# Where the MLP products of the plain tokens stand between the fronts, and which queue loads the first turned tokens

## The chip, the cores and the metric

The kernel runs on one core of one Trainium2 chip. The metric is device time in microseconds (us) of one execution. The kernel before took 865.07 us, the median of three runs (863.32, 865.07 and 866.03).

TensorE (PE) multiplies; PEld is its weight load. VectorE (DVE), ScalarE (ACT) and GpSimd (POOL) do the elementwise work, and SyncE (SP), ACT and POOL also start DMAs. Each of these takes its instructions strictly in its own order.

## What is computed

Linear attention with a decay per head, in blocks, then Fourier mixing, a layer norm and an MLP. Cut to what matters:

```
# q, k, v: 4 batches, 8 heads, 768 positions, 64 per head
x = attention(q, k, v, lam)            # reshaped to (4, 768, 512)
mixed = real(fft(fft(x, axis=1), axis=2))
u = x + mixed
un = (u - mean(u)) / sqrt(var(u) + 1e-06)
out = u + maximum(un @ w_ch1, 0) @ w_ch2   # 512 -> 2048 -> 512
```

All products are float32. The weights come as float64 words and are turned into float32 on the chip.

## The kernel before, in words

**Fronts.** For each of the 4 batches there is a front. `attn(b)` runs 6 chunks of 128 positions: the chunk's k and q are turned (L268, L273), multiplied (L292), masked by DVE (L296), multiplied with v (L324) and with the running state (L320), and turned back (L340). Then `fft_ln(b)` folds the chunk results by symmetry, and for that it gathers mirrored rows from DRAM (`mirror_a`, `mirror_b`, L415 to L431; the stores are on ACT's queue, the gathers on POOL's). `fold_a` and `fold_b` are DVE work; the L483 products need them. Then come three groups t = 1, 2, 0: the L496 to L501 products, DVE sums, and `norm(t)`: statistics on DVE (L513, L514), 1/sqrt on POOL (L517, L518), and the normalized rows `un` on DVE (L530).

**Plain and late tokens.** A group is 256 tokens. `ORDER` lists the 12 groups of (batch, group). The first four, `PLAIN`, are turned by TensorE (L535) and go through `mlp`: 16 times four L599 products with a ReLU on ACT or DVE in turns (L605, L607), and L613 products back to 512 columns, added to `u` (L620 to L625). The other eight, `LATE`, are turned by DVE (L540), stored to DRAM in four small stores each half (`utd`, L544, on SP's queue) along with `u` itself (`ud`, L550).

**The end.** After the last front, `combine_weights(0)` forms sums and differences of weight blocks on DVE (L663, tiles `w1s` and `w2s`); `load_u(0)` loads the first two late groups (tile `ur`, L670); `combine_weights(1)` changes two weight blocks in place. Then `late(j)` does two groups at a time with seven block products where eight would be usual (L686, L733), four times, to the end of the program. The first of them needs `ur`, and from its third product on `us`, which DVE makes from `ur` (L676 to L679).

**What sets the order.** Each generator yields an estimate of the work it has just recorded, and `weave` lets a second generator record its work while the first one's clock runs ahead, by a ratio. The ratios come from `t_front`, `t_mlp`, `t_rest` and `t_back` (L800 to L825). The four plain MLPs (`half[0]`, `half[1]`, `mlp(*PLAIN[3])`) are the filler between the steps of the fronts, since a front is a chain from engine to engine. `t_back` is what of these MLPs is to be spent on the fronts; the number taken off it stays behind the last front, and is drained by `run(weave(combine_weights(0), back, 1.5))` and `run(back)`. A scheduler then settles each engine's order; on the chip it is fixed.

Of the kernel before, what the change touches and what calls it, by code (L numbers as in the profile page):

```python
# [76 lines left out]
def kernel(  # L77
# [10 lines left out]
    nc = tc.nc  # L88
# [4 lines left out]
    NC = S // C  # L93
# [45 lines left out]
    def new(pool, shape, tag, **kw):  # L139
        cnt[0] += 1  # L140
        return pool.tile(shape, F32, tag=tag, name=f"{tag}{cnt[0]}", **kw)

    def psum_a(shape):
        return new(pa, shape, "pa")
# [79 lines left out]
    def weights():  # L224

        for h in range(2):
            for f in range(h * DFF // 2, (h + 1) * DFF // 2, WP):
                for c in range(KO):
                    load_weights(w1[:, c, f:f + WP], w1v[:, c, f:f + WP])
                    yield 1.0  # L230
            for c in range(h * FO // 2, (h + 1) * FO // 2):
                load_weights(w2[:, c, :], w2v[:, c, :])
                yield 1.0
# [7 lines left out]
    def attn(b):  # L241

        head = attn_in(b, 0)
        for c in range(NC):
            yield from head
            head = attn_in(b, c + 1) if c < NC - 1 else ()
            yield from attn_out(b, c, head)
# [146 lines left out]
    uts, utd, ud = {}, {}, {}  # L394
# [42 lines left out]
    def fold_b(b):  # L437

        sets = []
        tt = nc.vector.tensor_tensor  # L440
        for a, n in enumerate(BLK):
            fold_x(b, a, n, 0, xs[b, a][0:n], xs[b, HC + a][0:n])
            e, o = eo[b][a]
            nc.scalar.copy(e[0:n, :, HM:HM + 1], e[0:n, :, DM - 1:DM])

            am, bm = e[0:n, :, W:2 * W], o[0:n, :, W:2 * W]
            lo, hi = e[0:n, 0, 0:HM + 1], e[0:n, 1, 0:HM + 1]
            tt(am[:, 0, 0:HM + 1], lo, hi, op=ALU.add)
            tt(am[:, 1, 0:HM + 1], lo, hi, op=ALU.subtract)

            lo, hi = am[:, :, 0:QM], am[:, :, HM:QM:-1]
            tt(e[0:n, :, 0:QM], lo, hi, op=ALU.add)
            tt(e[0:n, :, QM:HM], lo, hi, op=ALU.subtract)
            lo, hi = o[0:n, 0, 1:HM], o[0:n, 1, 1:HM]
            tt(bm[:, 0, 1:HM], lo, hi, op=ALU.subtract)
            tt(bm[:, 1, 1:HM], lo, hi, op=ALU.add)
            lo, hi = bm[:, :, 1:QM + 1], bm[:, :, HM - 1:QM - 1:-1]
            tt(o[0:n, :, 0:QM], lo, hi, op=ALU.subtract)
            tt(o[0:n, :, QM:HM], lo, hi, op=ALU.add)
            sets.append((e, o))  # L460
        eo.pop(b)

        def piece(a, i, n):

            c0 = W + QM if i == 4 else QM * (i % 2)
            return sets[a][i in (2, 3)][0:BLK[a], n, c0:c0 + (1 if i == 4 else QM)]

        return piece

    def fft_ln(b):  # L470
# [1 line left out]
        fold_a(b)  # L472
        yield 3.0
        piece = fold_b(b)
        yield 6.0


        for i in range(5):
# [30 lines left out]
        def norm(g):  # L509
            mv = new(np_, [128, G, 2], "mv")  # L510
            for i in range(G):
                stt = new(np_, [128, 6], "stt")
                nc.vector.bn_stats(stt, xs[b, TT[g][i]])  # L513
                nc.vector.bn_aggr(mv[:, i, :], stt)  # L514
            ve = new(np_, [128, G], "ve")
            rs = new(np_, [128, G], "rs")
            nc.gpsimd.tensor_scalar(ve, mv[:, :, 1], EPS, None, op0=ALU.add)  # L517
            nc.gpsimd.tensor_tensor(rs, ve, mhalf, op=ALU.pow)  # L518
            yield 1.0
            plain = (b, g) in PLAIN  # L520
            if plain:
                ut = uts[b, g] = new(up, [128, KO, G * 128], "ut")
            else:

                to = utd[b, g] = dram.tile([128, KO, G * 128], F32, name=f"utd{b}{g}")
            for i in range(G):
                un = new(np_, [128, DM], "un", bufs=1)
                u = xs[b, TT[g][i]]
                for o, x in ((un[:, 0:HM], u[:, 0:HM]), (un[:, HM:DM], u[:, DM - 1:HM - 1:-1])):
                    nc.vector.tensor_scalar(o, x, mv[:, i, 0:1], rs[:, i:i + 1],  # L530
                                            op0=ALU.subtract, op1=ALU.mult)
                if plain:
                    pt = psum_a([128, KO, 128])
                    for c in range(KO):
                        nc.tensor.transpose(pt[:, c, :], un[:, 128 * c:128 * c + 128], ident)  # L535
                    nc.scalar.copy(ut[:, :, 128 * i:128 * i + 128], pt)
                else:

                    uq = new(ep, [128, DM], "e")
                    nc.vector.transpose(uq, un)  # L540
                    for r in range(0, 128, 32):
                        dst = to[:, :, 128 * i + r:128 * i + r + 32].rearrange("(a d) c n -> d c a n", d=32)
                        src = uq[r:r + 32].rearrange("p (c a n) -> p c a n", c=KO, n=32)
                        nc.sync.dma_start(dst, src)  # L544
                yield 0.7
            if plain:
                return
            for T in TT[g]:
                ud[b, T] = dram.tile([128, DM], F32, name=f"ud{b}{T}")
                nc.sync.dma_start(ud[b, T], xs.pop((b, T)))  # L550
# [31 lines left out]
    PLAIN, LATE = ORDER[:4], ORDER[4:]  # L582
# [80 lines left out]
                V.tensor_tensor(o[:, i:i + n // 2], x[:, i:i + n // 2], y[:, i:i + n // 2], op=op)  # L663
                yield 1.3

    def load_u(j):

        r = s2.u[j] = new(s2.up, [128, 2, KO, G * 128], "ur", bufs=2)
        for h, (b, g) in enumerate(LATE[2 * j:2 * j + 2]):
            nc.sync.dma_start(r[:, h], utd[b, g])  # L670

    def late(j):
        r = s2.u.pop(j)
# [54 lines left out]
        if 2 * j + 2 < len(LATE):  # L728
            load_u(j + 1)
# [36 lines left out]
    def front(b):  # L766
        yield from attn(b)
        yield from fft_ln(b)

    def weave(lead, other, ratio):  # L770

        t_lead = t_other = 0.0
        for d in lead:
            t_lead += d
            while t_other < t_lead * ratio:
                d = next(other, None)
                if d is None:
                    return t_lead + sum(lead)
                t_other += d
                yield d  # L780
            yield d
        return t_lead

    def run(gen):
        return sum(gen)

    def part(gen, n):
        for d in gen:
            yield d
            n -= d  # L790
            if n <= 0:
                return

    def chain(gens):
        for g in gens:
            yield from g

    NW = 2 * KO * DFF // WP
    w = weights()
    t_chunk = 7.3  # L800
    t_front = NC * t_chunk + 10.0 + 7.0 + 5.7 + 3 * 2.4
    t_mlp = FO * 1.7 + G * 4 * 3.4

    def beside(lead, t, other, t_other):
        return weave(lead, part(other, t_other), t_other / t)

    att1, mix = attn(1), fft_ln(0)
    run(beside(attn(0), NC * t_chunk, w, 0.25 * NW))

# [3 lines left out]
    run(beside(part(att1, t_chunk), t_chunk, w, 0.03 * NW))  # L813
    next(mix)
    run(part(att1, 0.5 * t_chunk))
    run(beside(mix, 20.0, beside(att1, 3.5 * t_chunk, w, 0.19 * NW), 0.19 * NW + 2.5 * t_chunk))

    half = [[mlp(b, g, h * FO // 2, (h + 1) * FO // 2) for b, g in PLAIN[:3]] for h in range(2)]
    fr = chain([att1, fft_ln(1)] + [front(b) for b in range(2, B)])
    t_rest, t_back = 3 * t_front - 5 * t_chunk, len(PLAIN) * t_mlp - 25.0  # L820
    t_half = 1.5 * t_mlp
    run(beside(beside(chain(half[0]), t_half, w, 0.5 * NW), t_half + 0.5 * NW, fr, t_rest * t_half / t_back))
    run(w)
# [3 lines left out]
    s2.wp = ctx.enter_context(tc.tile_pool(name="ws", bufs=1, side="left", reuse_waits="tile"))  # L827
    s2.up = ctx.enter_context(tc.tile_pool(name="us", bufs=1, side="left", reuse_waits="tile"))
    s2.u = {}
    load_u(0)  # L830
    run(weave(combine_weights(0), back, 1.5))
    run(back)
    plain_end.close()
# [37 lines left out]
```

## Time and profile before

| | |
|---|---|
| median of three runs | 865.07 us |
| the profiled execution's own time | 862.61 us |
| its span in the profile | 860.2 us |
| mean granted TensorE clock | 0.978 |
| PE busy | 804.9 us (94%) |
| DVE busy | 445.6 us (52%) |
| ACT busy | 181.4 us (21%) |
| POOL busy | 80.3 us (9%) |
| DMA | 68.87 MB, mean 80 GB/s |

Times in the views count from the span's start. In the view of waits, a line names the engine and line that waited, and after the arrow the engine and line whose work ended the wait; then total us, times, longest. In the timeline, a line has start, duration, engine, line, operation, tiles and count, and in brackets the idle time of the engine just before and what ended it. In the view of windows, the columns are the stretch, its length, the busy us of PE, PEld, DVE, ACT and POOL, the granted TensorE clock (1.00 is full speed), the share of DMA time and GB/s.

One thing to know for counting: every float32 product of the program appears twice in the trace. The order of a built program lists 256 L599 products, the profile 512.

### The profile page before, as it was taken

Reading aid. Unit: us, or ns where it says so; the run is one execution under the profiler, and the core shown is the slowest. Engines: PE = TensorE matmul, PEld = TensorE weight load, DVE = VectorE, ACT = ScalarE, POOL = GpSimd, SP = SyncE. Lnnn points to the kernel's source line nnn. Section 1 sums busy time; section 2 is a strip of 40 time slices with the busy share of each in tenths; the row PEclk is TensorE's granted clock in tenths of the full one; section 3 lists DMA queues with packets and bytes.
Section 4 is the critical chain, followed back from the end, with each engine's and each line's share of the span. In section 5 each row is a group of like instructions: output and inputs, shape, how many; then the busy total and the mean of one; then the engine's idle time right before and its main releaser. Section 6 shows DMA issues by size and latency. Waiting matters only on the chain.

```text
span 860.2 us, 11694 instructions
## 1 busy us (share of the span) xinstructions
PE 804.9 (94%) x4608; PEld 643.4 (75%) x4608; DVE 445.6 (52%) x1030; ACT 181.4 (21%) x436; POOL 80.3 (9%) x102
## 2 busy tenths in 40 slices
PE   5977698999999999999983999999999999999998
PEld 4766575767676767678632888888888888888886
DVE  6969988786712683226396553135511553135411
ACT  3653532314412211221100220012100220012100
POOL 2221132010101011111000000000000000000000
PEclk9998899999999999999995999999999999999999
DMA  9967362136724037511136001010111000110010
GB/s 242 251 163 194 98 190 74 50 104 190 184 51 133 32 68 160 127 64 55 31 80 195 1 1 62 37 49 1 50 50 49 1 1 13 38 49 1 1 37 24
DMA packets 126683, 68.87 MB, mean 80 GB/s; under 512 B 111150, under 2 KB 112174, under 8 KB 126630
## 3 DMA queue, kind: packets, MB, share of 16 engines
q1 hardware_dynamic: 121920, 56.72, 25.4%
q0 software_dynamic: 2112, 6.69, 2.4%
q10 hardware_dynamic: 2598, 4.73, 1.5%
q8 instruction: 36, 0.59, 0.3%
q14 instruction: 17, 0.14, 0.1%
HBM read 48.72 MB, written 19.40 MB: 79 GB/s over the span
## 4 chain that ended last, share of the span: by engine, by line
PE 79%; DVE 11%; DMA 3%; issue 3%; ACT 2%; POOL 1%; SPq 1%; DVEq 0%; POOLq 0%
PE p L686 23%; PE p L733 23%; PE pm L599 9%; PE pm L613 8%; PE pa L292 3%; PE pa L483 3%; PE pa L324 3%; DMA x<-xb,ix 2%; PE pa L320 1%; PE pa L340 1%; PE pa L268 1%; DVE sc L296 1%; PE pa L307 1%; PE pa L273 1%; DVE stt L513 1%
## 5 line engine op out<-in xcount | busy, mean ns | idle before, releaser
L599 PE MATMUL pm<-ut,w 128*128 128x256 f32 x512 | 119.8, 383 | 0.0
L613 PE MATMUL pm<-w,hr 128*128 128x512 f32 x256 | 117.3, 603 | 0.0
L686 PE MATMUL p<-ur,w 128*128 128x256 f32 x384 | 96.2, 386 | 17.6 <-DMA ur<-utd 17.6
L599 PEld LDWEIGHTS pm<-ut,w 128*128 128x128 f32 x512 | 94.3, 190 | 14.3 <-issue 2.7
L686 PEld LDWEIGHTS p<-ur,w 128*128 128x128 f32 x384 | 74.6, 194 | 28.8 <-issue 18.4
L613 PEld LDWEIGHTS pm<-w,hr 128*128 128x128 f32 x256 | 47.2, 192 | 49.3 <-issue 48.7
L686 PE MATMUL p<-us,w1s 128*128 128x256 f32 x256 | 66.6, 383 | 0.0
L733 PE MATMUL p<-w,hs 128*128 128x256 f32 x256 | 58.0, 380 | 0.5 <-DVE y L754 0.5
L733 PE MATMUL p<-w,ha 128*128 128x256 f32 x256 | 57.9, 379 | 0.0
L733 PE MATMUL p<-w2s,hs 128*128 128x256 f32 x256 | 57.9, 379 | 0.0
L686 PEld LDWEIGHTS p<-us,w1s 128*128 128x128 f32 x256 | 49.3, 193 | 6.8
L733 PEld LDWEIGHTS p<-w,hs 128*128 128x128 f32 x256 | 48.6, 190 | 7.5 <-DVE y L754 0.9
L733 PEld LDWEIGHTS p<-w2s,hs 128*128 128x128 f32 x256 | 48.7, 190 | 6.6
L733 PEld LDWEIGHTS p<-w,ha 128*128 128x128 f32 x256 | 48.7, 190 | 6.6
L588 POOL DMA_INDIRECT out_dram<-y,ix x12 | 12.6, 1049 | 405.5 <-DVE y L759 352.6
L713 ACT COPY ha<-p 128x256 f32<-128x256 f32 x32 | 11.9, 372 | 176.2 <-PE p L686 176.2
L292 PEld LDWEIGHTS pa<-qT,kT 64*128 64x128 f32 x384 | 28.6, 204 | 16.4 <-ACT qT L275 8.0
L292 PE MATMUL pa<-qT,kT 64*128 64x128 f32 x384 | 33.7, 305 | 6.2 <-ACT qT L275 5.8
L724 DVE TENSOR_TENSOR ha<-p,ha 128x256 f32<-128x256 f32 x32 | 13.6, 425 | 46.5 <-ACT ha L723 46.5
L296 DVE TENSOR_TENSOR sc<-pa,decay 128x512 f32<-128x512 f32 x48 | 31.6, 684 | 11.4 <-PE pa L292 11.2
L324 PE MATMUL pa<-sc,v 128*64 128x128 f32 x384 | 30.7, 286 | 5.1 <-DVE sc L296 5.0
L264 POOL TENSOR_TENSOR kd<-k,decay 128x512 f32<-128x512 f32 x20 | 22.9, 1147 | 115.9 <-PE pa L307 79.5
(144 smaller groups left out, 1140.4 us busy)
## 6 DMA issues: line engine op xcount, KB each, us to landing
raw<-in_moe_w_ch_dram SPq DMA_DIRECT2D x32, 512.0 KB, 4.7
k<-in_k_dram SPq DMA_DIRECT2D x24, 256.0 KB, 4.2
q<-in_q_dram SPq DMA_DIRECT2D x24, 256.0 KB, 5.3
v<-in_v_dram SPq DMA_DIRECT2D x24, 256.0 KB, 3.9
ud<-x SPq DMA_DIRECT2D x16, 256.0 KB, 2.5
utd<-e SPq DMA_DIRECT2D x64, 64.0 KB, 2.2
ur<-utd SPq DMA_DIRECT2D x8, 512.0 KB, 6.7
u<-ud SPq DMA_DIRECT2D x16, 256.0 KB, 2.7
```

Source lines behind the costliest of these rows:

```text
L264: nc.gpsimd.tensor_tensor(kd, kt, kpow, op=ALU.mult)
L292: mm(pss[hi][:, hp, :], lhsT=kT[HD[hi], hp, :], rhs=qT[HD[hi], hp, :], start=True, stop=True)
L296: nc.vector.tensor_tensor(t, pss[hi], decay[:, hi::2, :], op=ALU.mult)
L324: mm(po[HD[hi], hp, :], lhsT=vt[:, 2 * hp + hi, :], rhs=sc[hi][:, hp, :], start=(c == 0 and hp == 0), stop=(hp == HP - 1), skip_group_chec ...
L483: mm = nc.tensor.matmul(ps[0:m, n, :], lhsT=piece(a, i, n), rhs=cs[0:rows, a, i in (2, 3), n, :], start=(a == 0), stop=(a == 1))
L588: nc.gpsimd.indirect_dma_start(out=out.rearrange("b s d -> (b s) d"), out_offset=row_of(2 + HC * (b + 1) + T - HC), in_=y[:, :], in_offset ...
L599: nc.tensor.matmul(ps, lhsT=w1[:, c, 128 * fc:128 * fc + 128], rhs=ut[:, c, :], start=(c == 0), stop=(c == KO - 1))
L613: nc.tensor.matmul(ps, lhsT=hr[(fc - f0) // 4][:, fc % 4, 128 * i:128 * i + 128], rhs=w2[:, fc, :], start=(fc == f0), stop=(fc == f1 - 1))
L686: nc.tensor.matmul(ps, lhsT=s2.A[a][:, kt, 128 * i:128 * i + 128], rhs=U[b][:, kt, :], start=(first and kt == 0), stop=(kt == 1), skip_gro ...
L713: nc.scalar.copy(a11, two(X))
L724: V.tensor_tensor(a22, two(Z), a22, op=ADD)
L733: nc.tensor.matmul(ps, lhsT=h[a][:, s, i, :], rhs=s2.B[b][:, i, :], start=(first and i == 0), stop=(i == HF - 1), skip_group_check=True)
```

## The change

Five numbers and one queue:

- 45.0 in place of 25.0 is taken off `t_back`, so that more of the plain MLPs is left for after the fronts.
- `t_front` counts 13.0 for the fold where it had 10.0, and `fft_ln` yields 9.0 in place of 6.0 between fold and products, except for batch 0.
- Between the statistics and the normalized rows of the very first group, `norm` yields 5.0 in place of 1.0; the lead's time in that weave is 24.0 in place of 20.0.
- `load_u` takes a queue, and the first call uses ACT's in place of SP's.

```
         piece = fold_b(b)
-        yield 6.0
+        yield 6.0 if b == 0 else 9.0
...
             nc.gpsimd.tensor_tensor(rs, ve, mhalf, op=ALU.pow)
-            yield 1.0
+
+            yield 5.0 if (b, g) == PLAIN[0] else 1.0
...
-    def load_u(j):
+    def load_u(j, queue=nc.sync):
...
-            nc.sync.dma_start(r[:, h], utd[b, g])
+            queue.dma_start(r[:, h], utd[b, g])
...
-    t_front = NC * t_chunk + 10.0 + 7.0 + 5.7 + 3 * 2.4
+    t_front = NC * t_chunk + 13.0 + 7.0 + 5.7 + 3 * 2.4
...
-    run(beside(mix, 20.0, beside(att1, 3.5 * t_chunk, w, 0.19 * NW), 0.19 * NW + 2.5 * t_chunk))
+    run(beside(mix, 24.0, beside(att1, 3.5 * t_chunk, w, 0.19 * NW), 0.19 * NW + 2.5 * t_chunk))
...
-    t_rest, t_back = 3 * t_front - 5 * t_chunk, len(PLAIN) * t_mlp - 25.0
+    t_rest, t_back = 3 * t_front - 5 * t_chunk, len(PLAIN) * t_mlp - 45.0
...
-    load_u(0)
+
+    load_u(0, nc.scalar)
```

Lines after L515 stand one or two further down in the changed kernel (L599 is L600, L613 is L614, L670 is L671, L686 is L687). The order of the two built programs, engine by engine, shows where instructions moved; the prediction quotes it. In it a tile has its name and a running number, and a row that stands for several like instructions ends in their count.

- At the end of the last front, 16 products of L599 and then 32 of L613 stand behind the front's last product (L499), where 16 of L613 stood.
- Early in the program, the turning of the first plain rows (L535) stands behind the next chunk's L292 products, where it stood ahead of them.
- In the last two fronts, the fillers between chunks and folds are dealt out anew.

## The prediction

> **What bounds the kernel now.** I read the page first, then who waited for whom on PE, then the stretch around the longest wait.
>
> ```profile
> span 860.2 us, 11694 instructions
> PE 804.9 (94%) x4608; PEld 643.4 (75%) x4608; DVE 445.6 (52%) x1030; ACT 181.4 (21%) x436; POOL 80.3 (9%) x102
> PE p L686 <- DMA ur<-utd: 17.6, 1, 17.6
> PE pa L535 <- DVE un L530: 8.2, 4, 6.4
> PE pa L483 <- DVE fe L452: 5.0, 3, 3.8
> ```
>
> PE is busy for all but 55.3 us, and three causes hold 30.8 us of these. The largest is one wait: PE, done with the plain MLPs, waits for the first turned tokens. The windows around it show what it costs besides.
>
> ```profile
> 440.00:448.20 8.20, 8.20 (x20) 3.33 (x18) 7.51 (x9) 0.00 (x0) 0.66 (x1) 1.00 0.21 36
> 448.20:465.80 17.60, 0.03 (x2) 0.04 (x1) 14.48 (x17) 0.00 (x0) 1.79 (x1) 0.59 0.57 157
> 465.80:474.00 8.20, 8.20 (x24) 6.73 (x25) 3.45 (x7) 1.12 (x3) 0.00 (x0) 0.62 0.70 278
> 474.00:482.00 8.00, 8.00 (x39) 7.06 (x38) 4.75 (x14) 1.87 (x5) 0.00 (x0) 1.00 0.01 2
> ```
>
> DVE works through the wait, and PE starts again at a clock of 0.62. The timeline of this stretch, PE's rows and then SP's and DVE's:
>
> ```profile
> 433.91 0.38 PE L499 MATMUL pa<-dt,ys 128*1 128x128 f32 x2
> 434.22 14.00 PE L613 MATMUL pm<-w,hr 128*128 128x512 f32 x32
> 465.79 3.75 PE L686 MATMUL p<-ur,w 128*128 128x256 f32 x8 [17.57 <-DMA ur<-utd]
> 473.24 1.89 PE L686 MATMUL p<-ur,w 128*128 128x256 f32 x8
> 474.97 1.03 PE L686 MATMUL p<-ur,w1s 128*128 128x256 f32 x4
> 457.53 2.59 SPq L544 DMA_DIRECT2D utd<-e  x4
> 461.37 1.85 SPq L670 DMA_DIRECT2D ur<-utd  x4
> 459.66 0.42 DVE L624 TENSOR_TENSOR y<-pm,x 128x256 f32<-128x256 f32 x1
> 460.32 2.36 DVE L663 TENSOR_TENSOR w<-w 128x1024 f32<-128x1024 f32 x2
> 467.03 0.69 DVE L676 TENSOR_TENSOR us<-ur 128x512 f32<-128x512 f32 x1 [4.35 <-DMA ur<-utd]
> ```
>
> The front's last product ends at 434.3, and only 13.8 us of products are left to PE. The load of `ur` (SP, 461.37) stands behind the last stores of turned tokens, which wait for DVE. DVE is done with the weight blocks at 462.7, 28.4 us after that product. So this stage is bound by DVE's chain and the queue behind it. At full clock eight records take 1.73 us (473.24 to 474.97), 0.216 each; the 20 records from 465.79 to 473.24 would take 4.3 us, not 7.45. The wait thus costs 17.6 + 3.1 = 20.7 us.
>
> **The change, part by part.**
>
> *More products kept (45.0 in place of 25.0).* On PE, from the front's last product (L499) to the first with `ur`, before:
>
> ```order
> L499 MATMUL pa_3678<-dt,ys_133 1x128
> L613 MATMUL pm_3706<-w_130,hr_3302 128x512 x4
> L613 MATMUL pm_3706<-w_130,hr_3400 128x512 x4
> L613 MATMUL pm_3706<-w_130,hr_3446 128x512 x4
> L613 MATMUL pm_3706<-w_130,hr_3497 128x512 x4
> L686 MATMUL p_3800<-ur_3737,w_129 128x256 x2
> ```
>
> and now, from just behind that product (pa_3632) on:
>
> ```order
> L600 MATMUL pm_3650<-ut_1675,w_129 128x256 x4
> L600 MATMUL pm_3676<-ut_1675,w_129 128x256 x4
> L600 MATMUL pm_3705<-ut_1675,w_129 128x256 x4
> L600 MATMUL pm_3711<-ut_1675,w_129 128x256 x4
> L614 MATMUL pm_3718<-w_130,hr_3422 128x512 x4
> L614 MATMUL pm_3718<-w_130,hr_3459 128x512 x4
> L614 MATMUL pm_3718<-w_130,hr_3537 128x512 x4
> L614 MATMUL pm_3718<-w_130,hr_3655 128x512 x4
> L614 MATMUL pm_3746<-w_130,hr_3422 128x512 x4
> L614 MATMUL pm_3746<-w_130,hr_3459 128x512 x4
> L614 MATMUL pm_3746<-w_130,hr_3537 128x512 x4
> L614 MATMUL pm_3746<-w_130,hr_3655 128x512 x4
> ```
>
> So 16 products of L600 and 32 of L614 now stand there, where 16 of the latter stood. Their prices, from the chain of waits in the middle of the fronts (eight records are four products):
>
> ```profile
> 226.14 3.44 PE pm L613 x8
> 259.63 1.73 PE pm L599 x8
> ```
>
> That is 4 x 1.73 + 8 x 3.44 = 34.4 us of cover. What must end under it is DVE's chain: 28.4 us, plus three more ReLUs (0.42 each, 1.3 us), plus the four `us` operations (0.69 each, 2.8 us) that the order puts ahead of the last `y`, less that `y` (0.8 us), plus 1.7 us, because only four L600 products now stand between the last two product groups of the front where 3.44 us stood. The sum is 33.4 us. All but 1 us of cover is used, so I take 20.2 us as gained, bounds 12 and 20.7: the low one if DVE is 5 us late and PE restarts at half clock (3.1 us again).
>
> *The load on ACT's queue.* On ACT, at the same place, now:
>
> ```order
> L562 COPY ds_3620<-pa_3612 128x2
> L608 ACTIVATE hr_3655<-pm_3650 128x256
> L671 DMA ur_3699<-utd_1741 128x1024
> L671 DMA ur_3699<-utd_1825 128x1024
> L608 ACTIVATE hr_3655<-pm_3705 128x256
> L714 COPY ha_3793<-p_3800 128x2x128
> ```
>
> The load is issued right behind the first of the kept ReLUs and no longer behind SP's stores. Behind it on ACT stands a ReLU (pm_3705) that the second row of products needs. The data it loads were stored in an earlier front, so I expect it to issue at once: cost nothing, hidden under products. Its worth is that `us` can be made under the cover; alone on SP it would land some 4 us after 461.37, still under most of 34.4 us. Of the new waits I cost only the first copy behind PE (L714), which wants the last `ud` stores landed. Those were issued between 460.1 and 461.4, right behind the four stores of the last turned half above, and take 2.5 us to land, so they stay inside the cover:
>
> ```profile
> ud<-x SPq DMA_DIRECT2D x16, 256.0 KB, 2.5
> ```
>
> *The spacing at the first norm.* Here PE idles 6.4 us for `un`:
>
> ```profile
> 95.89 0.63 ACT L275 COPY qT<-pa 128x512 f32<-128x512 f32 x1
> 101.65 0.73 DVE L530 TENSOR_SCALAR un<-x,mv,rs 128x256 f32<-128x256 f32 x2 [0.92 <-POOL rs L518]
> 102.20 1.09 PE L535 MATMUL pa<-ident,un 128*128 128x128 f32 x4 [6.36 <-DVE un L530]
> 95.85:102.20 6.35, 0.00 (x0) 0.03 (x1) 5.43 (x14) 2.61 (x6) 1.03 (x2) 0.82 0.51 124
> 102.20:110.30 8.10, 8.10 (x82) 7.03 (x82) 7.87 (x18) 2.29 (x6) 1.06 (x1) 0.72 0.01 3
> ```
>
> The next chunk's L292 products (some 1.1 us), now ahead of L535, can start at 96.6, when qT is there. But DVE is busy for 5.43 of these 6.35 us, and in its new order one mask product (L296) stands ahead of the second aggregate; so `un` comes no earlier than before, and some 4.6 us of idle are left. I take 2 us as gained: 1.1 for the products, 0.9 for products that ran at half clock and now don't. The bounds are nothing (DVE decides) and 8.6 us: the whole idle and 8.1 x (1 - 0.72) = 2.3 us of slow clock.
>
> The clock rows here weigh a rule. The Trainium skill (TensorE: Matmul & The Clock Gate, section What's actually happening) has the clock halve after at least one idle window of about 3.4 us, and the window runs freely. The mean of 0.82 over 6.35 us, with 1.00 before, agrees: at 1.00 first and 0.50 after, it fell some 4.1 us into the idle. By the rule an idle of 4.6 us still costs the half clock, one under 3.4 us would not, and the sum would be about 1.4 us better.
>
> *The fillers dealt out anew.* From 180 to 450 PE waited only for folds:
>
> ```profile
> PE pa L483 <- DVE fe L452: 1.1, 2, 1.0
> PE pa L483 <- DVE fe L448: 0.2, 1, 0.2
> ```
>
> With 20.7 us of filler gone from the fronts, the fold of batch 2 is the thin place. On PE between its last turning (L340) and its first fold product (L483), before:
>
> ```order
> L340 MATMUL pa_2530<-ident,oT_2522 128x128 x4
> L613 MATMUL pm_2524<-w_130,hr_2431 128x512 x4
> L613 MATMUL pm_2584<-w_130,hr_2353 128x512 x4
> L613 MATMUL pm_2584<-w_130,hr_2431 128x512 x4
> L599 MATMUL pm_2603<-ut_1271,w_129 128x256 x3
> L483 MATMUL pa_2597<-cs,fe_2471 128x193
> ```
>
> and now:
>
> ```order
> L340 MATMUL pa_2500<-ident,oT_2491 128x128 x4
> L600 MATMUL pm_2512<-ut_1187,w_129 128x256 x4
> L600 MATMUL pm_2527<-ut_1187,w_129 128x256 x4
> L600 MATMUL pm_2533<-ut_1187,w_129 128x256 x4
> L600 MATMUL pm_2565<-ut_1187,w_129 128x256 x4
> L614 MATMUL pm_2571<-w_130,hr_2428 128x512 x4
> L614 MATMUL pm_2571<-w_130,hr_2517 128x512 x4
> L614 MATMUL pm_2596<-w_130,hr_2428 128x512 x4
> L614 MATMUL pm_2596<-w_130,hr_2517 128x512 x4
> L483 MATMUL pa_2584<-cs,fe_2440 128x193
> ```
>
> There are more products, but the later ones free the buffer that the gather needs:
>
> ```profile
> 276.47 0.41 DVE L625 TENSOR_TENSOR y<-pm,x 128x256 f32<-128x256 f32 x1
> 277.15 1.15 POOL L429 DMA_INDIRECT x<-xb,ix  x1 [8.22 <-DVE y L625]
> 283.68 0.42 DVE L452 TENSOR_TENSOR fe<-fe 128x256 f32<-128x256 f32 x1
> 284.24 0.57 PE L483 MATMUL pa<-cs,fe 128*128 128x193 f32 x2
> ```
>
> From the end of that block (pm_2524, about 276.0) to the fold's result (284.1) were 8.1 us, covered by 8.2 us: 6.9 of L613 and 1.3 of L599. Now 6.9 us (pm_2596) stand behind the block that frees it (pm_2571), 1.2 us short; the second gather, freed by pm_2596, leaves another 1 us. I take 2.2 us lost. In batch 3 six L614 and twelve L600 products (10.4 us) stand at the like place, close to what the chain took, and I give it 0.3 us. Its last four chunks now have one L614 product each between them. One such chunk ran before without a gap, 6.07 us from L292 to L292, so they get 0.5 us:
>
> ```profile
> 353.25 1.16 PE L292 MATMUL pa<-qT,kT 64*128 64x128 f32 x16
> 358.37 1.02 PE L613 MATMUL pm<-w,hr 128*128 128x512 f32 x2
> 359.32 1.16 PE L292 MATMUL pa<-qT,kT 64*128 64x128 f32 x16
> ```
>
> Together 3 us lost, bounds 0 and 8 (a fold of 3.8 us idle, as batch 1 has in the waits above, at each of two batches). Batch 1's own fold keeps nearly the same fillers behind its last turning, so its 3.8 us stay; 0.
>
> **The sum.** -20.2 - 2 + 3 = -19.2 us. The profiled execution's own time is 862.61 us (860.2 of span and 2.4 around it), which gives 843.4. The median of the three runs, 865.07, is 2.5 above that execution, so I forecast 846 us.
>
> **The rivals.**
>
> *The folds starve.* The gathers come later than I reckon, and PE idles past the point where its clock falls: 8 us lost where I have 3, so 851. For it: the gather waits for DVE, which takes `y` in between its fold steps. Against it: only 1.3 us of waits in 270 us before. By the clock rule above, each idle over one window also costs slow products behind it.
>
> *The end's wait comes back in another form.* DVE's chain has 1 us of cover by my sum. If stores or ReLUs delay it by 5 us, PE stands 5 us and restarts at half clock, 3.1 us: 854. For it: the cover is thin. Against it: DVE ran through the whole stretch before without waiting for a store.
>
> *The clock holds where it fell.* If the early idle and batch 1's fold both shrink a little, their slow products go: 1.4 us at the first, and about 1.7 at the second (0.57 for 4 us in the row below): 843.
>
> ```profile
> 144.00:148.00 4.00, 4.00 (x10) 2.35 (x9) 4.00 (x11) 0.19 (x1) 0.00 (x0) 0.57 0.00 0
> ```
>
> *Slower: the fronts run bare.* The freed PE time cannot be used, because every chunk of batches 2 and 3 is held by its own chain. It decides the sign where a chunk loses 1.6 us: 12 of them then lose the 19.2 us. At 2.4 us each the time is 875. Against it: the bare chunk above lost nothing.
>
> *It does nothing.* The same number of products would be left for the end; the order shows 16 and 32 where 16 stood, so this is nearly excluded.
>
> **How the numbers follow.** Chances: forecast 0.58, starved folds 0.17, the end's wait again 0.08, clock held 0.12, slower 0.03, nothing 0.02. The range, 839 to 855, takes in starved folds, the returned wait and the held clock, with room at the low end for an early gain nearer its bound. About 0.3% (2.6 us) is what a measurement of this kernel can tell from no change. Faster by more: 0.95; within it: 0.02; slower: 0.03.
>
> **What would show it.** Right: the wait of L687 for `ur` under 2 us; clock 1.00 through the start of L687; the load on ACT's queue landed long before; an L536 wait near 4.6 us; L483 waits about 2 us more than before in batch 2. Wrong: a wait of L687 for DVE or a store over 3 us; new waits of L268, L292, L324 or L340 in batches 2 and 3 that sum to over 5 us; or a gap of the fold over 4 us with the clock below 1 behind it.

## The result, and the profile after

The changed kernel takes 844.07 us, the median of four runs (843.69 to 846.26); the kernel before took 864.20 beside it (four runs, 862.77 to 866.03). The ratio is 0.9771, with a 95% interval of 0.9744 to 0.9798. The forecast was 846 us, with 839 to 855 as its range. The profiled execution of the changed kernel took 844.24 us, 842.3 of them span.

The page of the changed kernel, its first line and the engines' busy time, and then its longest waits of PE from 104 us to the end of the fronts (engine and tile, releaser, total, times, longest):

```profile
span 842.3 us, 11685 instructions
PE 805.3 (96%) x4608; PEld 642.3 (76%) x4608; DVE 446.0 (53%) x1030; ACT 181.9 (22%) x436; POOL 77.2 (9%) x102
```

```profile
PE pa L536 <- DVE un L531: 6.4, 3, 4.6
PE pa L483 <- DVE fe L452: 4.1, 5, 1.2
PE pm L614 <- DVE hr L606: 1.3, 1, 1.3
PE pa L324 <- DVE sc L296: 0.7, 1, 0.7
```

PE's busy time is the same, 805 us; idle time is what went. The wait for `ur` is gone from the list. The folds' waits (L483) are 4.1 us in sum where they were 5.2, but spread: five short ones and none of 3.8. Two kinds are new: one wait for a ReLU and one for a chunk's masked scores.

The end of the fronts in the changed kernel, as a timeline, PE first and then the load on ACT's queue, SP's load and DVE's chain:

```profile
415.70 0.38 PE L499 MATMUL pa<-dt,ys 128*1 128x128 f32 x2
416.01 3.72 PE L600 MATMUL pm<-ut,w 128*128 128x256 f32 x16
419.92 3.72 PE L600 MATMUL pm<-ut,w 128*128 128x256 f32 x16 [0.19 <-DVE hr L606]
423.48 27.71 PE L614 MATMUL pm<-w,hr 128*128 128x512 f32 x64
451.03 1.89 PE L687 MATMUL p<-ur,w 128*128 128x256 f32 x8
455.34 1.03 PE L687 MATMUL p<-ur,w 128*128 128x256 f32 x4
418.05 0.81 ACTq L671 DMA_DIRECT2D ur<-utd  x2
445.31 0.98 SPq L671 DMA_DIRECT2D ur<-utd  x2
445.72 0.68 DVE L677 TENSOR_TENSOR us<-ur 128x512 f32<-128x512 f32 x1
448.66 0.69 DVE L679 TENSOR_TENSOR us<-ur,us 128x512 f32<-128x512 f32 x1
```

and the windows over the cover and over the first products behind it (start:end, length, busy time of PE, PEld, DVE, ACT and POOL, PE's granted clock, DMA share, GB/s):

```profile
416.00:451.00 35.00, 34.81 (x97) 18.18 (x97) 31.39 (x50) 0.77 (x2) 1.84 (x4) 1.00 0.53 140
451.00:455.30 4.30, 4.30 (x21) 3.78 (x20) 1.48 (x4) 0.74 (x2) 1.08 (x1) 1.00 0.50 191
```

PE has 35.0 us of products from its last one of the fronts (ended 416.08) to the first on `ur` (451.03). DVE is done with `us` at 449.35, 33.3 us after that product, so 1.7 us of cover are left over. (The first products that need `us` come another 1.7 us later, at 452.75.) The 20 records that took 7.45 us at a clock of 0.62 now take 4.31 (451.03 to 455.34) at 1.00. Wait and slow clock, 17.6 + 3.1 us, are both gone. Against that, the fronts should end 20.7 us earlier, because 20.7 us of products left them; they end 18.2 earlier (434.29 and 416.08).

Early in the program the changed kernel shows this: the first norm, the gather of batch 1, and its first fold product.

```profile
98.75 1.16 PE L292 MATMUL pa<-qT,kT 64*128 64x128 f32 x16 [0.97 <-ACT qT L275]
104.47 1.11 PE L536 MATMUL pa<-ident,un 128*128 128x128 f32 x4 [4.56 <-DVE un L531]
135.16 1.45 POOL L429 DMA_INDIRECT x<-xb,ix  x1 [4.75 <-DMA xb<-xn]
142.44 0.89 PE L483 MATMUL pa<-cs,fe 128*128 128x193 f32 x4 [0.86 <-DVE fe L452]
```

The idle before `un` is 4.56 us, as worked out beforehand. The gap of batch 1's fold, 3.84 us before, is 0.86, which was not foreseen. The gather ahead of it was being issued for 4.00 us before and is issued in 1.45 now. The kernel before, at the same place:

```profile
133.40 4.00 POOL L429 DMA_INDIRECT x<-xb,ix  x1 [6.33 <-DMA xb<-xn]
143.67 1.01 PE L483 MATMUL pa<-cs,fe 128*128 128x193 f32 x4 [3.84 <-DVE fe L452]
```

### The profile page after: what moved, and what is told of

Read it like the earlier page. It is cut to its first block, busy times and chain, and to the rows that moved or that the text cites. A ratio compares the mean times of both kernels' runs of the same rounds, so it can differ in the third digit from the quotient of the medians.

```text
span 842.3 us, 11685 instructions
## 1 busy us (share of the span) xinstructions
PE 805.3 (96%) x4608; PEld 642.3 (76%) x4608; DVE 446.0 (53%) x1030; ACT 181.9 (22%) x436; POOL 77.2 (9%) x102
## 3 DMA queue, kind: packets, MB, share of 16 engines
q0 software_dynamic: 2112, 6.69, 2.5%
## 4 chain that ended last, share of the span: by engine, by line
PE 80%; DVE 10%; issue 4%; DMA 3%; ACT 2%; POOL 1%; SPq 0%; POOLq 0%; DVEq 0%; ACTq 0%
PE p L734 23%; PE p L687 23%; PE pm L614 9%; PE pm L600 7%; PE pa L292 3%; PE pa L324 3%; PE pa L483 3%; PE pa L320 2%; PE pa L340 1%; DMA x<-xb,ix 1%; PE pa L268 1%; PE pa L307 1%; PE pa L273 1%; DVE stt L513 1%; DMA xb<-xn 1%
## 5 line engine op out<-in xcount | busy, mean ns | idle before, releaser
L600 PE MATMUL pm<-ut,w 128*128 128x256 f32 x512 | 119.8, 383 | 0.2 <-DVE hr L606 0.2
L614 PE MATMUL pm<-w,hr 128*128 128x512 f32 x256 | 116.1, 598 | 1.3 <-DVE hr L606 1.3
L600 PEld LDWEIGHTS pm<-ut,w 128*128 128x128 f32 x512 | 94.1, 190 | 15.6 <-issue 3.4
L687 PE MATMUL p<-ur,w 128*128 128x256 f32 x384 | 93.8, 379 | 0.0
L614 PEld LDWEIGHTS pm<-w,hr 128*128 128x128 f32 x256 | 46.6, 190 | 51.4 <-issue 48.6
L687 PEld LDWEIGHTS p<-ur,w 128*128 128x128 f32 x384 | 73.0, 190 | 10.3 <-issue 0.5
L687 PE MATMUL p<-us,w1s 128*128 128x256 f32 x256 | 65.7, 379 | 0.0
L687 PEld LDWEIGHTS p<-us,w1s 128*128 128x128 f32 x256 | 48.6, 190 | 6.6
L589 POOL DMA_INDIRECT out_dram<-y,ix x12 | 11.8, 987 | 408.4 <-DVE y L760 344.2
L292 PEld LDWEIGHTS pa<-qT,kT 64*128 64x128 f32 x384 | 29.2, 205 | 18.3 <-ACT qT L275 10.9
L292 PE MATMUL pa<-qT,kT 64*128 64x128 f32 x384 | 34.3, 306 | 8.0 <-ACT qT L275 7.5
L324 PE MATMUL pa<-sc,v 128*64 128x128 f32 x384 | 31.9, 288 | 4.5 <-DVE sc L296 4.5
L324 PEld LDWEIGHTS pa<-sc,v 128*64 128x64 f32 x384 | 23.4, 141 | 13.6 <-DVE sc L296 7.6
```

What stands on the lines that cost most here:

```text
L292: mm(pss[hi][:, hp, :], lhsT=kT[HD[hi], hp, :], rhs=qT[HD[hi], hp, :], start=True, stop=True)
L324: mm(po[HD[hi], hp, :], lhsT=vt[:, 2 * hp + hi, :], rhs=sc[hi][:, hp, :], start=(c == 0 and hp == 0), stop=(hp == HP - 1), skip_group_chec ...
L589: nc.gpsimd.indirect_dma_start(out=out.rearrange("b s d -> (b s) d"), out_offset=row_of(2 + HC * (b + 1) + T - HC), in_=y[:, :], in_offset ...
L600: nc.tensor.matmul(ps, lhsT=w1[:, c, 128 * fc:128 * fc + 128], rhs=ut[:, c, :], start=(c == 0), stop=(c == KO - 1))
L614: nc.tensor.matmul(ps, lhsT=hr[(fc - f0) // 4][:, fc % 4, 128 * i:128 * i + 128], rhs=w2[:, fc, :], start=(fc == f0), stop=(fc == f1 - 1))
L687: nc.tensor.matmul(ps, lhsT=s2.A[a][:, kt, 128 * i:128 * i + 128], rhs=U[b][:, kt, :], start=(first and kt == 0), stop=(kt == 1), skip_gro ...
```

## The experiments

Three questions were asked: which of the parts brings the gain; why batch 1's fold gap shrank; and how much cover the end can use. Medians and ratios are over the timed runs, always against the kernel before on the same chip (863.8 to 864.5 us in the three sets).

### Which part brings the gain at the end

**The kept products alone** (the kernel before with one number):

```
-    t_rest, t_back = 3 * t_front - 5 * t_chunk, len(PLAIN) * t_mlp - 25.0
+    t_rest, t_back = 3 * t_front - 5 * t_chunk, len(PLAIN) * t_mlp - 45.0
```

> The kernel before with 45.0 for 25.0 alone; the first load of ur stays on SP's queue, the spacing as before. Theory A (cover: the wait at the end is DVE's chain of 33 us behind the front's last product, less the products left there, here 34.5 us as in the change): 847 us, no wait of PE for ur over 2 us, because even on SP the load lands some 35 us after that product. Theory B (the load's place on SP's queue is what PE waited for): 857 us, the wait still over 8 us. Theory C (spacing makes most of the gain): 860 us or more.

It took 848.34 us, ratio 0.9818 (0.9793 to 0.9842), 15.9 less than before. No wait for `ur` or `us` is left, though the load stands on SP. Its longest waits in the fronts behind 200 us:

```profile
PE pa L483 <- DVE fe L452: 3.1, 3, 1.9
PE pm L613 <- DVE hr L605: 1.0, 1, 1.0
PE pa L324 <- DVE sc L296: 0.7, 1, 0.7
```

So the one number brings the end's 20.7 us and costs some of it in the fronts: 3.8 us by PE's idle from 200 us to their end (1.3 us before, 5.1 here), 4.8 by the medians.

**The load on ACT's queue alone:**

```
-    load_u(0)
+    load_u(0, nc.scalar)
```

> The kernel before with the load of ur on ACT's queue alone. Theory A: ur is there early, but DVE makes us only behind the last weight blocks, so PE's wait moves from the load to us and shrinks by some 4 us: 860 us. Theory B: 846 to 850 us, the wait gone. Theory C: 864 us.

861.01 us, ratio 0.9968 (0.9953 to 0.9983). The load is issued at 433.94, and PE does its first eight records on `ur` at once; then it waits all the same:

```profile
433.94 0.51 ACTq L670 DMA_DIRECT2D ur<-utd  x1
450.74 1.89 PE L686 MATMUL p<-ur,w 128*128 128x256 f32 x8
467.39 7.16 PE L686 MATMUL p<-ur,w 128*128 128x256 f32 x24 [14.76 <-issue]
463.01 2.34 DVE L663 TENSOR_TENSOR w<-w 128x1024 f32<-128x1024 f32 x2
466.60 0.69 DVE L679 TENSOR_TENSOR ur<-ur 128x512 f32<-128x512 f32 x1
```

The row names "issue" as releaser. PE starts again 0.10 us after DVE's L679, which changes a block of `ur` in place (it ended at 467.29); it is one of the four operations L676 to L679 that DVE starts only once its weight blocks are done (465.35). In the change with 25.0, below, the profile names this very operation as the releaser. So behind the wait for the load, which the profile of before puts down to a DMA, stood a second limit almost as late: DVE's chain.

**The change with the load on SP:** `load_u(0)` in the changed kernel.

> The change with the load of ur back on SP's queue. Theory A: 844 to 846 us, at most 2 us of wait, since the cover of 34.5 us hides the later load too. Theory B: 855 us or more. Theory C: 844 us.

842.66 us, ratio 0.9769 (0.9748 to 0.9790). The end waits once, for 0.8 us:

```profile
PE p L687 <- DVE y L626: 0.8, 1, 0.8
```

With the cover there, the queue is worth nothing that these runs resolve: the changed kernel's 844.07 is not better than this.

**The change with 25.0:**

> The change with 25.0 for 45.0: ACT's queue and the spacing alone, 13.8 us of products behind the front's last product. Theory A: the wait at the end is back, some 13 to 16 us and with slow products behind it; with 4 us from the queue and 2 to 4 us from the spacing, 857 us. Theory B: 846 us. Theory C: 846 us.

860.85 us, ratio 0.9954 (0.9935 to 0.9972). The wait at the end is back (11.8 + 2.1 us, for `y` and for the block of `ur` that DVE changes), and more was lost than expected. What was lost besides lies in batch 2's fold: an idle of 2.08 us (286.11 to 288.19), and behind it a clock that stays low.

```profile
286.00:288.20 2.20, 0.12 (x2) 0.01 (x1) 2.20 (x8) 0.20 (x1) 0.00 (x0) 1.00 0.00 0
288.20:302.00 13.80, 13.80 (x42) 10.92 (x43) 1.61 (x5) 2.51 (x5) 0.00 (x0) 0.53 0.00 0
302.00:304.00 2.00, 2.00 (x14) 1.89 (x13) 0.00 (x0) 0.57 (x3) 0.00 (x0) 0.81 0.00 0
```

At 0.53 over 13.8 us and 0.81 over the next 2, some 6.9 us of products' time went to that clock (13.8 x 0.47 + 2.0 x 0.19). That is one execution of 862.45 us. The twelve of this kernel lie between 854.69 and 862.52, and their mean clocks fall from 0.982 to 0.969 with the time, so the low clock need not last as long in each of them.

### Who shrank batch 1's fold gap

**The spacing at the first norm alone**, on the kernel before:

```
-            yield 1.0
+            yield 5.0 if (b, g) == PLAIN[0] else 1.0
-    run(beside(mix, 20.0, ...
+    run(beside(mix, 24.0, ...
```

> The kernel before with the spacing behind the first norm alone (5.0 for 1.0, 24.0 for 20.0). Question: which part shrank batch 1's fold gap, 3.8 us before and 0.9 us with the whole change (it is 0.9 also with the change less the 45.0, and 3.95 with 45.0 alone, so 45.0 is not it). Theory A (the early spacing does both): the wait of L535 for un goes from 6.4 to about 4.6, the fold gap of batch 1 to about 1, the first gather's issue of batch 1 from 4.0 to about 1.5 us, PE's clock behind that fold stays at 1.00; the wait for ur stays near 17. Time 864 - 2 - 4.6 = about 858. Theory B (the early spacing moves only the early idle): fold gap stays 3.8, 862 to 863. Theory C (no gain at all, its products come from what stood elsewhere): 864.

857.91 us, ratio 0.9927 (0.9907 to 0.9947), 5.9 less. Theory A holds in each of its points: the wait for `un` is 4.57 us, the gather's issue 1.45, the fold gap 0.78, and behind it the clock stays up:

```profile
135.36 1.45 POOL L429 DMA_INDIRECT x<-xb,ix  x1 [4.75 <-DMA xb<-xn]
142.57 0.89 PE L483 MATMUL pa<-cs,fe 128*128 128x193 f32 x4 [0.78 <-DVE fe L452]
```

```profile
144.00:148.00 4.00, 4.00 (x15) 1.78 (x15) 4.00 (x12) 0.20 (x1) 0.00 (x0) 1.00 0.00 0
```

**The spacing at the folds alone:**

```
-        yield 6.0
+        yield 6.0 if b == 0 else 9.0
-    t_front = NC * t_chunk + 10.0 + 7.0 + 5.7 + 3 * 2.4
+    t_front = NC * t_chunk + 13.0 + 7.0 + 5.7 + 3 * 2.4
```

> The kernel before with the spacing behind the second fold step alone (9.0 for 6.0 in batches 1 to 3, t_front 13.0). Theory A (the early spacing shrinks batch 1's gap): gap here stays near 3.8 with a clock of about 0.57 behind it, early idle 6.4, wait for ur 17 to 18, folds of batches 2 and 3 below 1 us; time 863 to 865. Theory B (the spacing of the fold shrinks it, as the words of the change say): gap about 1, time about 859.5.

871.40 us, ratio 1.0089 (1.0064 to 1.0113): slower by 7.6 us, which neither theory had. Batch 1's gap stays (4.1 us in the waits), as A said. But batch 2's fold, which had no wait over 1 us before, now has one of 2.04, and the clock falls behind it; the end's wait is 19.5 us where it was 17.6.

```profile
PE p L686 <- DMA ur<-utd: 19.5, 1, 19.5
PE pa L483 <- DVE fe L452: 7.3, 3, 4.1
```

```profile
295.43 3.01 PE L483 MATMUL pa<-cs,fe 65*128 65x193 f32 x12 [2.04 <-DVE fe L452]
```

```profile
295.00:297.00 2.00, 1.57 (x9) 1.58 (x10) 2.00 (x7) 0.29 (x1) 0.00 (x0) 0.93 0.00 0
297.00:303.00 6.00, 6.00 (x20) 5.51 (x19) 0.04 (x1) 1.25 (x4) 0.00 (x0) 0.50 0.00 0
303.00:305.00 2.00, 2.00 (x10) 0.98 (x9) 0.00 (x0) 0.79 (x2) 0.00 (x0) 0.86 0.00 0
```

The idle is 2.0 us, the slow clock 3.4 (2 x 0.07 + 6 x 0.50 + 2 x 0.14), the longer wait at the end 1.9: together 7.3 of the 7.6 us. So an edit meant to put more work ahead of the folds' products took work away from one place in them. In the kernel before, two short groups of L483 products (291.33 and 292.01, 0.49 and 0.82 us) stood just ahead of those of L483 that now wait; here no products of L483 stand between the last fillers and them.

**The change without the spacing at the first norm:**

> The change without the spacing behind the first norm. Theory A (the early spacing shrinks batch 1's gap): early idle 6.4, batch 1's gap back near 3.8 with its slow clock, end's wait absent; time 844 + 2 + 4.6 = about 850. Theory B (the fold's spacing does it): gap about 0.9, time 846. Theory C: the early parts are worth nothing, 844.

850.15 us, ratio 0.9842 (0.9820 to 0.9864); early idle 6.36 us, batch 1's gap 3.91, the gather's issue 3.99. Theory A.

**The change without the spacing at the folds:**

> The change without the spacing at the folds. Theory A (the early spacing shrinks batch 1's gap): gap stays near 0.9; with 6.0 less filler is asked for at the folds of batches 2 and 3, whose gaps grow from 1.2 and 1.8 to 2 to 4 us each; time 844 to 849. Theory B (the fold's spacing shrinks batch 1's gap): gap 3.8 with its slow clock and the same at batches 2 and 3, 850 to 856.

841.95 us, ratio 0.9754 (0.9729 to 0.9779). The gap of batch 1 stays at 0.88 (theory A), but those of batches 2 and 3 did not grow as A said: they are 1.10 and 1.57 us, about what the whole change has. In the change, too, the folds' spacing brings nothing.

**Two ReLUs taken from DVE**, on the kernel with the early spacing alone. Why is the gather's issue short there? In it DVE does a ReLU from PSUM (L605) while POOL issues the gather; before, it runs only weight blocks from SBUF to SBUF there. So that ReLU and the next were given to ACT:

```
-            if fc % 2:
+            if fc % 2 and cnt[0] not in (300, 304):
```

> The kernel before with the early spacing (857.9, gather 1.45, gap of batch 1's fold 0.8), and two of batch 1's ReLUs, which DVE did from PSUM while the first gather was being issued, now done by ACT. DVE then runs only operations from SBUF to SBUF there. Theory A (the gather's issue on POOL is held while DVE runs such operations back to back, and gets through at one that reads PSUM): the issue takes 3 to 4 us, the fold gap grows to 2.5 to 4, the clock halves behind it, time 861 to 865. Theory B (DVE's work doesn't matter to the issue; the early spacing only moves it away from something else): 1.3 to 1.5 us, the gap 0.8 or less because DVE has two operations fewer, time 857 to 858.

860.89 us, ratio 0.9963 (0.9945 to 0.9982), 3.0 above the kernel that it edits (the two were timed in different sets, and the intervals of their ratios just touch). DVE has less to do and the gather takes three times as long. DVE and POOL in that stretch, and PE behind it:

```profile
136.45 4.60 POOL L429 DMA_INDIRECT x<-xb,ix  x1 [4.75 <-DMA xb<-xn]
136.86 0.42 DVE L215 TENSOR_SCALAR e<-raw 128x512 uint16<-128x512 uint16 x1
139.41 0.68 DVE L222 SCALAR_TENSOR_TENSOR w<-w,e 128x512 f32<-128x512 f32 x1
147.64 1.03 PE L483 MATMUL pa<-cs,fe 128*128 128x193 f32 x4 [3.90 <-DVE fe L452]
```

```profile
148.00:152.00 4.00, 4.00 (x12) 2.20 (x10) 4.00 (x12) 0.20 (x1) 0.00 (x0) 0.57 0.00 0
```

The issue ends at 141.05, 0.96 us after DVE's last weight operation (140.09). In the kernel with the early spacing, the issue of 135.36 ended 0.62 us after the ReLU:

```profile
135.78 0.41 DVE L605 TENSOR_SCALAR hr<-pm 128x256 f32<-128x256 f32 x1
```

Theory A holds in the gather and the gap, and the slow clock comes back with them. The time came out just under what A gave.

### How much cover the end can use

**The early spacing and the kept products, without the other two edits:**

> The kernel before with the early spacing and the 45.0 only: no spacing at the folds, the load on SP. Theory A (the four edits act apart from each other, and the folds' spacing and the queue are worth nothing or less): 864 - 5.9 - 15.5 = 842 to 843, the gaps of the folds 0.9 (batch 1), about 1.1 and 1.6, no wait at the end over 1 us. Theory B (the load's queue is needed once the folds' spacing is gone): a wait for ur of 3 us or more at the end, 846 to 849.

843.16 us, ratio 0.9758 (0.9737 to 0.9778); no wait at the end of 0.5 us or more, fold gaps 0.80, 0.98 and 1.58. Theory A. These two edits carry the whole gain. By themselves they gain 15.9 and 5.9 us, together 21.3. The folds' spacing loses 7.6 alone and nothing that shows beside the kept products. Those deal the fillers out anew; that this is why was not tried by itself. Neither this kernel nor the change without the folds' spacing can be told from the change itself by these intervals.

**35.0 in place of 45.0, in the change:**

> The change with 35.0 for 45.0: 24.1 us of products behind the front's last one instead of 34.4. Theory A (the end's wait is DVE's chain less this cover, 1 for 1): with a chain of 28 us (as the change with 25.0 showed: 11.8 + 2.1 of wait over 13.8 of cover) the wait is about 4, with my 33.4 us about 9; and where it is over 2 us the clock halves behind it, 2 to 3 us more. Time 849 to 856. Theory B (25.0 to 45.0 is a step, because only one load's place decides): no wait, 844 to 846.

847.27 us, ratio 0.9809 (0.9787 to 0.9831).

```profile
447.95 1.89 PE L687 MATMUL p<-ur,w 128*128 128x256 f32 x8
455.89 2.04 PE L687 MATMUL p<-us,w1s 128*128 128x256 f32 x4 [6.05 <-DVE us L678]
457.73 2.03 PE L687 MATMUL p<-ur,w 128*128 128x256 f32 x4
```

The wait is there, 6.05 us, and four records behind it take 2.0 us in place of 1.0. The front's last product ended at 423.88; so DVE's chain was 32.0 us (to 455.89), against 24.1 us of cover and 1.9 of products that need only `ur`. That is A's mechanism, between its two ends. The median is under A's range. The end loses 7.9 us here (6.05 of wait, 1.9 of slow clock). PE idles 2.5 us less in the fronts (2.8 us from 200 us to their end, 5.3 in the change), but 1.7 us of that go to a slow clock behind batch 3's fold. PE also starts its early idle 1.3 us sooner (96.44 and 97.78), ahead of anything this edit moves.

**65.0:**

> The change with 65.0 for 45.0: 53.5 us of products behind the front's last one. The end can gain nothing more, 19 us of products more leave the fronts. Theory A (thin places pay, a little each): waits of batches 2 and 3 grow from 5 us to 8 to 12, 847 to 852. Theory B (every chunk of the fronts runs bare, 1.6 us and more each): 855 to 870. Theory C (the fronts need none of it): 843 to 845.

848.72 us, ratio 0.9829 (0.9807 to 0.9851), 4.7 above the change. The time is A's, the place is not. PE's waits from 104 to 420 us:

```profile
PE pa L483 <- DVE fe L452: 5.2, 4, 2.6
PE pa L324 <- DVE sc L296: 3.5, 4, 1.7
```

The longest is again batch 1's fold, 2.62 us where the change has 0.86, behind a gather that took 2.20 us to issue. At L324 a chunk of batch 2 waits 1.12 us (181.43) and one of batch 3 1.69 (315.07). Most chunks still run without a gap.

## Why the prediction was right, point by point

**The end's wait: right in size and in cause.** -20.2 was forecast, the rows give -20.7. DVE's chain was put at 33.4 us and took 33.3; the cover at 34.4, and it was 35.0. That DVE's chain bounds this stage even with the load out of the way is shown by two runs: the load alone, brought forward by 27 us, left 14.8 us of wait, and with 35.0, where the load is early too, PE waits 6.05 us for `us`. That the cover alone left no wait fits either cause.

**The load on ACT's queue: right at nothing.** 842.66 without it, 844.07 with it. Without the cover it is worth 3.2 us (0.9968).

**The first norm: the idle right, its worth too high.** 4.6 us of idle were left, as said. I put 2 us on it; from the start of PE's idle to the first product on `un` 6.35 us became 6.69, with 1.16 us of L292 done inside, which is 0.8. The 0.9 us of slow clock did not come back: the mean clock from the start of the idle to the end of the slow stretch is 0.76 before (95.85 to 110.30) and 0.77 after (97.78 to 112.57).

**Batch 1's fold: wrong.** The step that failed reads "Batch 1's own fold keeps nearly the same fillers behind its last turning, so its 3.8 us stay; 0". It looked only at what PE has to do. The early spacing moved DVE's order too: a ReLU came to stand inside the gather's issue, the issue went from 4.0 to 1.45 us, the gap from 3.84 to 0.86, and the half clock behind it (0.57 for 4 us) went. That is 3.0 + 1.7 = 4.7 us, and the early spacing alone measures 5.9 in all. The slow clock there is the second half of the rival "The clock holds where it fell", at 0.12; the 3.0 us of idle no rival had.

**The fillers dealt anew: right in kind, too small.** +3 was forecast. PE's idle from 200 us to the end of the fronts, in the windows of the two kernels:

```profile
200.00:434.20 234.20, 232.87 (x1479) 167.35 (x1477) 113.26 (x252) 51.73 (x125) 30.83 (x38) 1.00 0.40 101
```

```profile
200.00:416.00 216.00, 210.72 (x1380) 153.63 (x1376) 111.15 (x247) 52.23 (x125) 30.35 (x36) 1.00 0.41 100
```

It grew from 1.3 to 5.3 us, +4.0. Batch 2's fold lost 1.2 us where I had 2.2; the two gaps of batch 3's fold make 1.8 where I added 0.3 to 0.95; a bare chunk lost 2.0 (a ReLU 1.3, L324 0.7) where I had 0.5. What I had not asked is what the folds' own spacing is worth. By itself it makes the kernel 7.6 us slower; in the change no cost of it can be told (841.95 us without it, 844.07 with it).

**The sum.** -20.7 - 0.8 - 4.7 + 4.0 = -22.2 by the rows. The medians differ by 20.1, and the spans of the two profiled executions, from which the rows come, by only 17.9 (860.2 and 842.3). So 4.3 us were lost that no row above holds. Some 2 of them lie ahead of the early idle, which PE starts at 95.85 us in the profiled execution before and at 97.78 after. Scatter alone does that: in the five kernels without the early spacing this point lies between 95.85 and 98.67, in the nine with it between 95.43 and 99.11, though within each group PE comes to it by the same order of instructions. The other 2 us are not assigned. So my -19.2 came near the measured -20.1 partly by luck: the missed 4.7 us, and 0.5 more at the end, were made up for by two terms that were each 1 us too good (the first norm and the fillers) and by some 2 us that the rows don't assign.

**The rivals.** Returned wait: shown at 35.0, so the cover's margin decides; at 45.0 it is 1.7 us. Starved folds: not in the change, but it is what the folds' spacing does alone. Bare fronts: at 65.0 the loss is 4.7 us, not 1.6 us a chunk.

## What to carry to other kernels

When PE waits for a load, look for what the loaded data meet next: here the load was 27 us early in one run and PE waited for the engine behind it. Price a cover by the chain that must end under it, and stop there: 10 us less brought 6 us of wait back, 20 us more cost 4.7 us elsewhere. And when work is moved on PE, read the order of the other engines at the same place as well; the second largest gain of this change came from where one ReLU stands in DVE's order.

## What the runs showed of the hardware

**A gather's issue on POOL is held by DVE.** The same gather of batch 1 took 4.00 us to issue before, and 3.99 to 4.60 in every kernel in which DVE ran its weight blocks without a break there, ending 0.96 or 0.97 us after the last of them. It took 1.28 to 1.46 where a ReLU from PSUM came in between, and 2.20 in the kernel with 65.0, where the ReLU came 1.17 us after the start of the issue (135.90 and 134.73). In all of these, too, the issue ended 0.96 or 0.97 us after the weight operation just ahead of that ReLU. So in these runs it matters when the run of weight operations is first broken behind the issue's start; the next gather, which nothing held, took 0.95 us to issue in the kernel before. The Trainium skill (SBUF — State Buffer, section SBUF: two separate sides) says that a DMA from POOL's queue needs its descriptors written by POOL, which is locked out of the port pair that the two engines share while DVE runs an operation in a 2-port mode. The trace agrees in that the issue waits for DVE. Which of DVE's kinds of weight operation holds it, these runs don't separate.

**An idle of about 2 us can halve the clock, and one of 2.6 us need not.** Behind an idle of 2.04 us (the folds' spacing alone) the clock was 0.50 for 6.8 us, behind one of 2.08 us (the change with 25.0) for some 13.7. Idles of 1.58 us (the two edits), 1.87 us (the kept products alone) and 2.62 us (65.0) left it at 1.00, and one of 1.25 us (394.87 to 396.12, batch 3's fold in the kernel with 35.0) was followed by a fall some 2 us later:

```profile
396.00:398.00 2.00, 1.88 (x11) 1.88 (x12) 1.74 (x6) 0.51 (x1) 0.00 (x0) 1.00 0.00 0
398.00:400.00 2.00, 2.00 (x8) 1.62 (x7) 0.00 (x0) 0.50 (x1) 0.00 (x0) 0.55 0.00 0
```

The prediction's rule, that an idle under 3.4 us would not cost the half clock, does not hold here. The length of the idle alone doesn't decide between 1.25 and 2.62 us. In the three that fell, the idle is followed by a run of 12 records of L483 with 65 rows; in the three that did not, by L483 with 128 rows and products of the MLP among them. No run separates that from the moment at which the idle falls. So a gap of some 2 us cost nothing besides itself here, or 3.4 us more, or 6.9.
